# A static tile of 128 rows per expert between the passes of a switch-routed MoE, with a hint for the code of the next pass

## The chip, the cores and the metric

The kernel runs on one core of one Trainium2 chip. The metric is the device time of one execution in microseconds; of the kernel before there are three timed runs, 733.85, 734.2 and 734.55 us, and one further execution that the hardware profiler recorded.

## The reference

Attention with a band and a few global keys, and behind it a mixture of experts that sends each token to one expert. All data are f32.

```python
# attention: B 4, H 8, S 768, D 64; keys 0..7 are global, else the last 96
scores = q @ k.T / sqrt(D) + bias        # bias = -slope[h] * distance
a = softmax(where(keep, scores, -1e9))
x = (a @ v).transpose(0, 2, 1, 3).reshape(3072, 512)
# experts: E 8, DM 512, F 1024
expert_idx = argmax(x @ w_gate, axis=1)
gate_w = softmax(x @ w_gate)[arange(N), expert_idx]
for e in range(E):
    mask = expert_idx == e
    out[mask] = gate_w[mask, None] * (maximum(x[mask] @ w1[e], 0) @ w2[e])
```

How many of the 3072 tokens go to which expert is known only on the chip, at run time.

## The kernel before

The first 207 us or so are the attention (`banded`). It leaves every block of tokens in rows `xr` together with the routing logits `lg`; `choose` and `dispatch` pick the expert of each token and scatter the rows into `xs_dram`, sorted by expert (L205, POOL). The weights of experts 0 and 1 (2 MB each for w1 and w2) are loaded by SP into two slots while the attention is still running (`fetch`, L718).

The experts' work comes in two kinds.

*Static tiles* have exactly 128 rows and the same code whatever the routing. `x_in_s` transposes the gathered rows into `xsT` (PE L762, DVE L763), `up_s` makes 64 matmuls of 128 columns (PE L771) with two relu's on ACT (L775), `down_s` makes 16 matmuls of 512 columns (PE L781), a multiplication by the gate on DVE (`ys`, L783) and one scatter to the output on POOL (L728). Before, only experts 0 and 1 have such a tile, and both are worked off ahead of the passes, under the tail of the dispatch.

*Passes* take the remaining rows of each expert, all experts in turn (`passes`). A pass is a switch over 14 widths, 0, 128, 160 and so on to 512 columns; for every width there is a body of code of its own, and PE, ACT, DVE and POOL each jump to the body whose number stands in the table `form`. SP has no switch. A body (`one_pass`) has an up phase, 8 groups of 8 matmuls (as the trace records them: two for each f32 matmul of the program) into `ph` (PE L874) with a relu into `hT` on ACT (L876), and a down phase, 4 times 16 recorded matmuls into `py` (PE L881; four 128-column blocks `d` of the output, 8 chunks `f` each), a copy to `yT` on ACT (L883), and `back`: transposes on PE (L862) and gated copies into `y` on DVE (L864, L868). At its end POOL scatters `y` to the output (L728). In between the body transposes the next expert's gathered rows (`x_in`, PE L840, DVE L841), up to four tiles of 128, the last of them just before the last `back`, and `x_meta` takes over token numbers and gates on DVE (L845, L847). With this run's tokens the widths are 352, 288, 384, 416, 384, 416, 416 and 288 for experts 0 to 7.

Behind each pass come the gathers of the expert after next on POOL (`gathers`, L721) and its weights on SP (`fetch`). Behind pass 0 there is also `judge`, one small matmul (L952) whose result decides at the very end whether a general path has to do the work again; it never does here.

PE's order of work is that of the program text (a manual schedule for PE); the other engines' instructions are placed by the scheduler, so that gathers for later passes may stand further ahead than in the text. At the head of each body of a switch a hint names the place behind the switch.

Of the kernel before, what the change touches and what calls it, by code (L numbers as in the profile page):

```python
# [9 lines left out]
F32 = mybir.dt.float32  # L10
# [10 lines left out]
def kernel(  # L21
# [659 lines left out]

    NS = 2
    TP = 4
# [3 lines left out]
    class Experts:  # L687
        def __init__(self, stack, rt, psum):
            self.rt = rt
            ps_s, ps_t, ps_o, ps_r = self.psum = psum  # L690
            self.wpool = stack.enter_context(tc.tile_pool(name="wpool", bufs=1))
            self.pool = stack.enter_context(tc.tile_pool(name="tab", bufs=1))
            self.w1 = [self.wpool.tile([P, NDC, F], F32, name=f"w1_{i}") for i in range(2)]
            self.w2 = [self.wpool.tile([P, NFC, DM], F32, name=f"w2_{i}") for i in range(2)]
# [4 lines left out]
            self.grow_s = T([P, NS], I32, name="grow_s")  # L699
            self.inv_s = T([P, NS], I32, name="inv_s")  # L700
# [4 lines left out]
            self.xs = [T([P, XW], F32, name=f"xs{i}") for i in range(NS)]  # L705
            self.xsT = [T([P, NDC, P], F32, name=f"xsT{i}") for i in range(NS)]
            self.hsT = T([P, NFC, P], F32, name="hsT")
            self.ys = T([P, DM], F32, name="ys")
            self.tos = T([P, NS], I32, name="tos")
# [26 lines left out]
        def early(self):  # L736
# [4 lines left out]
            inv = T([P, NS], F32, name="inv_sf")  # L741
            nc.vector.tensor_scalar(inv[:], cnt[:], iota_p[:, 0:1], None, ALU.is_le)
            row = T([P, NS], F32, name="row_s")
            nc.vector.tensor_scalar(row[:], ebase[:, 0:NS], iota_p[:, 0:1], None, ALU.add)
            nc.vector.scalar_tensor_tensor(self.grow_s[:], inv[:], float(2 ** 22), row[:], ALU.mult, ALU.add)
            nc.vector.tensor_scalar(self.inv_s[:], inv[:], float(2 ** 30), None, ALU.mult)
# [8 lines left out]
            for j in range(NS):  # L755
                self.gather(self.xs[j][:], self.grow_s[:, j:j + 1])


        def x_in_s(self, j):
            pt = self.t[j % 2]  # L760
            for c in range(NDC):
                nc.tensor.transpose(pt[:, c, :], self.xs[j][:, ts(c, P)], ident[:])  # L762
            nc.vector.tensor_copy(out=self.xsT[j][:], in_=pt[:])  # L763
            nc.vector.tensor_tensor(self.tos[:, j:j + 1], self.xs[j][:, DM + 1:DM + 2].bitcast(I32),
                                    self.inv_s[:, j:j + 1], ALU.bitwise_or)

        def up_s(self, j):
            for f in range(NFC):
                ph = self.ph[f // 4 % 2][:, 0, :]
                for c in range(NDC):  # L770
                    nc.tensor.matmul(ph[:, ts(f % 4, P)], lhsT=self.w1[j][:, c, ts(f, P)],  # L771
                                     rhs=self.xsT[j][:, c, :], start=(c == 0), stop=(c == NDC - 1),
                                     skip_group_check=True)
# [4 lines left out]
        def down_s(self, j):  # L778
            py = self.py[j % 2]
            for f in range(NFC):  # L780
                nc.tensor.matmul(py[:], lhsT=self.hsT[:, f, :], rhs=self.w2[j][:, f, :],  # L781
                                 start=(f == 0), stop=(f == NFC - 1))
            nc.vector.tensor_scalar(self.ys[:], py[:], self.xs[j][:, DM:DM + 1], None, ALU.mult)  # L783
            self.scatter(self.ys[:], self.tos[:, j:j + 1])


        def begin(self, stack):

            ps_s, ps_t, ps_o, ps_r = self.psum
            pool = stack.enter_context(tc.tile_pool(name="pass", bufs=1))  # L790
            self.xg = [pool.tile([P, TP, XW], F32, name=f"xg{i}") for i in range(2)]
# [7 lines left out]
            self.t = [ps_t.tile([P, TP, P], F32, tag="t", name=f"pt{i}") for i in range(2)]  # L799
# [3 lines left out]
        def clear(self, i):  # L803
            nc.vector.memset(self.xg[i][:], 0.0)

        def table(self):
# [8 lines left out]
            nc.vector.tensor_scalar(self.inv_i[:], inv[:], float(2 ** 30), None, ALU.mult)  # L815

            steps_i = T([P, E], I32, name="steps_i")
            nc.vector.scalar_tensor_tensor(steps_i[:], cnt[:], float(GN - 1), self.lim[:],  # L818
                                           ALU.add, ALU.subtract)
            nc.vector.tensor_scalar(steps_i[:], steps_i[:], GN.bit_length() - 1, None,  # L820
                                    ALU.logical_shift_right)
            steps = T([P, E], F32, name="steps")
# [26 lines left out]
        def one_pass(self, e, n, between):  # L849

            w1t, w2t, xT, hT, y = self.w1[e % 2], self.w2[e % 2], self.xT[e % 2], self.hT, self.y[e % 2]
# [26 lines left out]
            for d in range(NDC if n else 0):  # L878
# [7 lines left out]
                if d == 1:  # L886
# [9 lines left out]
        def passes(self, after_first):  # L896
            PEs = (PE, mybir.EngineType.Activation, mybir.EngineType.DVE, mybir.EngineType.Pool)
            _, forms = nc.values_load_multi_w_load_instructions(
                self.form[0:1, 0:E], engines=PEs, min_val=0, max_val=len(WIDTHS) - 1,
                skip_runtime_bounds_check_because="the table has no other forms")  # L900
            for e in range(E):
                index = {eng: forms[e] for eng in PEs}
                for i in tc.Switch(index, len(WIDTHS)):
                    more = []
                    if e + 1 < E:
                        self.x_meta(e + 1)
                        more = [lambda: (self.x_in(e + 1, 0), self.x_in(e + 1, 1)),
                                lambda: self.x_in(e + 1, 2), lambda: self.x_in(e + 1, 3)]
                    self.one_pass(e, WIDTHS[i], more)
                if e + 2 < E:  # L910
                    self.gathers(e + 2)
                    self.fetch(e + 2)
                if e == 0:
                    after_first()
# [4 lines left out]
    with ExitStack() as stack, tc.manual_schedule(engines={PE}):  # L919
# [8 lines left out]
        ex.clear(0)  # L928
# [29 lines left out]
    with tc.If(flag > 0):  # L958
# [36 lines left out]
```

## Time and profile before

| | |
|---|---|
| timed runs, median of 3 | 734.2 us (733.85 to 734.55) |
| profiled execution | 733.7 us |
| its span | 731.9 us |
| mean granted TensorE clock | 0.928 |
| PE busy | 578.0 us, 4093 instructions |
| DVE, ACT, POOL busy | 178.2, 126.1, 103.8 us |

The span is the time from the first to the last recorded instruction; 1.8 us of the execution lie around it. PE, DVE, ACT and POOL are the engines for matmuls, vector work, activations and general work; PEld is PE's weight load, SP issues most of the loads. "Busy" counts instructions that do work; an engine that waits for another is idle, and where the profile shows nothing that it waited for, the idle time is put down to "issue". Busy PE says nothing about its speed, which is why the granted clock is given beside it.

### The profile page before, as it was taken

The page shows a single profiled execution, that of the slowest core. Times are in us where ns is not written, and L with a number is a line of the kernel's source. Part 1 is how long each engine was busy: PE and PEld are TensorE (multiplying, and loading weights), DVE is VectorE, ACT ScalarE, POOL GpSimd, SP SyncE. Part 2 cuts the span into 40 slices and gives each one's busy share as a digit, 9 for nine tenths or more (in the row PEclk, how much of TensorE's full clock was granted, in tenths as well). Part 3 has the DMA queues.
Part 4 walks back from the last instruction along what each step waited for, and adds up shares of the span by engine and source line. Part 5 has one row for each costly group of instructions (what it writes and reads, how often), then busy time and mean ns, then how long its engine had stood idle before and what let it go on. Part 6 is the DMA issues. An engine that isn't in the chain of part 4 may idle for free.

```text
span 731.9 us, 10117 instructions
## 1 busy us (share of the span) xinstructions
PE 578.0 (79%) x4093; PEld 389.7 (53%) x4093; DVE 178.2 (24%) x499; ACT 126.1 (17%) x225; POOL 103.8 (14%) x148
## 2 busy tenths in 40 slices
PE   3898697997999499489489499948948985896890
PEld 2786576785876256357245345524524552454660
DVE  6565555664660101101101100110110020011010
ACT  1444243533410010010010011001001100100100
POOL 2002203105006300210300120040021002002001
PEclk9999999999999699789799889979979997998995
DMA  8888975566104203413603422060351304001001
GB/s 188 234 249 222 274 193 155 141 157 183 37 2 151 79 0 116 158 46 116 191 6 116 155 55 83 33 212 0 116 162 32 114 22 149 0 1 52 0 4 36
DMA packets 98473, 77.49 MB, mean 106 GB/s; under 512 B 79355, under 2 KB 79355, under 8 KB 98305
## 3 DMA queue, kind: packets, MB, share of 16 engines
q1 hardware_dynamic: 90240, 56.63, 26.7%
q0 software_dynamic: 6704, 18.98, 7.9%
q8 instruction: 56, 0.92, 0.6%
q14 instruction: 113, 0.92, 0.5%
q10 hardware_dynamic: 1360, 0.04, 0.1%
HBM read 61.45 MB, written 12.89 MB: 102 GB/s over the span
## 4 chain that ended last, share of the span: by engine, by line
PE 67%; issue 15%; DVE 8%; ACT 3%; DMA 2%; POOL 1%; ACTq 1%; another core or an unknown queue 0%; DVEq 0%; POOLq 0%
PE ph L874 25%; PE py L881 22%; PE po L358 4%; PE sp L336 4%; ACT hT L876 2%; PE pt L225 2%; PE pt L862 2%; PE pr L369 2%; PE pt L840 2%; PE px L380 2%; DVE p L347 2%; DMA xs_dram<-xr,slot_i 1%; DVE y L864 1%; PE pr L374 1%; PE ph L771 1%
## 5 line engine op out<-in xcount | busy, mean ns | idle before, releaser
L874 PE MATMUL ph<-xT,w 128*128 128x416 f32 (+3 forms) x512 | 188.0, 523 | 80.3 <-issue 60.7
L874 PEld LDWEIGHTS ph<-xT,w 128*128 128x128 f32 x512 | 103.6, 209 | 162.0 <-issue 97.8
L881 PE MATMUL py<-hT,w 128*128 128x416 f32 (+3 forms) x512 | 162.3, 473 | 0.0
L881 PEld LDWEIGHTS py<-hT,w 128*128 128x128 f32 x512 | 95.5, 190 | 55.5 <-issue 27.7
L728 POOL DMA_INDIRECT out_dram<-y,to x27 | 26.3, 976 | 393.4 <-DVE y L868 293.0
L876 ACT ACTIVATE hT<-ph 128x416 f32<-128x416 f32 (+3 forms) x64 | 30.5, 477 | 269.0 <-PE ph L874 253.7
L348 ACT ACTIVATE p<-p 128x1024 f32<-128x1024 f32 (+1 forms) x48 | 47.0, 983 | 86.8 <-DVE p L347 79.6
L841 DVE COPY xT<-pt 128x512 f32<-128x512 f32 x32 | 21.2, 685 | 165.9 <-PE pt L840 165.9
L864 DVE TENSOR_TENSOR y<-pt,gate 128x384 f32<-128x384 f32 (+1 forms) x32 | 16.3, 508 | 181.0 <-PE pt L862 180.9
L347 DVE SCALAR_TENSOR_TENSOR p<-sp,other 128x1024 f32<-128x1024 f32 x40 | 47.5, 1216 | 13.3 <-remote 9.8
L336 PE MATMUL sp<-qt,kt 64*128 64x128 f32 x448 | 40.5, 292 | 10.4 <-DVE p L347 7.2
L358 PE MATMUL po<-p,vt 128*64 128x128 f32 x448 | 41.2, 284 | 5.7 <-issue 5.6
L883 ACT COPY yT<-py 128x416 f32<-128x416 f32 (+3 forms) x32 | 14.9, 465 | 165.5 <-PE py L881 165.5
L336 PEld LDWEIGHTS sp<-qt,kt 64*128 64x128 f32 x448 | 33.4, 203 | 11.9 <-issue 11.2
L721 POOL DMA_INDIRECT xg<-xs_dram,grow x32 | 32.6, 1020 | 34.4 <-issue 33.8
L358 PEld LDWEIGHTS po<-p,vt 128*64 128x64 f32 x448 | 28.5, 142 | 8.6 <-issue 8.6
L205 POOL DMA_INDIRECT xs_dram<-xr,slot_i x24 | 23.8, 990 | 38.9 <-DVE steps_i L818 30.4
L840 PE MATMUL pt<-ident,xg 128*128 128x128 f32 x128 | 19.1, 285 | 10.2 <-DVE xT L841 4.7
L336 PE MATMUL sp<-qt,ka 64*128 64x128 f32 x256 | 26.6, 285 | 0.0
L358 PE MATMUL po<-p,va 128*64 128x128 f32 x256 | 25.7, 279 | 0.0
L369 PE MATMUL pr<-p,one_in 128*32 128x128 f32 x704 | 24.2, 276 | 0.0
L840 PEld LDWEIGHTS pt<-ident,xg 128*128 128x128 f32 x128 | 15.3, 146 | 15.0 <-DVE y L868 5.6
(148 smaller groups left out, 421.3 us busy)
## 6 DMA issues: line engine op xcount, KB each, us to landing
w<-in_moe_w_dram SPq DMA_DIRECT2D x32, 1024.0 KB, 6.4
raw_q<-in_q_dram SPq DMA_DIRECT2D x24, 256.0 KB, 3.2
raw_k<-in_k_dram SPq DMA_DIRECT2D x24, 256.0 KB, 4.0
vt<-in_v_dram SPq DMA_DIRECT2D x24, 256.0 KB, 3.8
va<-vt SPq DMA_DIRECT2D x16, 192.0 KB, 3.6
va<-vt SPq DMA_DIRECT2D x16, 64.0 KB, 3.0
xg<-xs_dram,grow POOLq DMA_INDIRECT x32
out_dram<-y,to POOLq DMA_INDIRECT x27
```

Of the source, the lines that this page charges most:

```text
L205: d = nc.gpsimd.indirect_dma_start(out=xs_dram[:], out_offset=bass.IndirectOffsetOnAxis(ap=slot_i[:, u:u + 1], axis=0), in_=xr[:, u, :].bi ...
L336: nc.tensor.matmul(sp[:, a, j, t, :], lhsT=kt[r, 2 * g + j, :], rhs=qts[n][r, 2 * g + j, :], start=True, stop=True, skip_group_check=True)
L347: nc.vector.scalar_tensor_tensor(z, sc, QS, bi, ALU.mult, ALU.add)
L348: nc.scalar.activation(z, z, AF.Exp)
L358: nc.tensor.matmul(po[D * a:D * a + D, m, :], lhsT=vt[:, 2 * m + a, :], rhs=ps[n][m // 2][:, a, m % 2, t, :], start=(x == 0), stop=(x == l ...
L369: nc.tensor.matmul(pr[GW * m:GW * m + GW, 0, :], lhsT=one_in[:, a, :], rhs=ps[n][m // 2][:, a, m % 2, t, :], start=(x == 0), stop=False, s ...
L721: nc.gpsimd.indirect_dma_start(out=dst.bitcast(I32), out_offset=None, in_=xs_dram[:], in_offset=bass.IndirectOffsetOnAxis(ap=idx, axis=0), ...
L728: d = nc.gpsimd.indirect_dma_start(out=out[:], out_offset=bass.IndirectOffsetOnAxis(ap=idx, axis=0), in_=src, in_offset=None, bounds_check ...
L840: nc.tensor.transpose(pt[:, c, :], x[:, t, ts(c, P)], ident[:])
L874: nc.tensor.matmul(ph, lhsT=w1t[:, c, ts(f, P)], rhs=xT[:, c, 0:n], start=(c == 0), stop=(c == NDC - 1), skip_group_check=True)
L876: nc.scalar.activation(hT[:, f, 0:n], ph, AF.Relu)
L881: nc.tensor.matmul(py, lhsT=w2t[:, f, ts(d, P)], rhs=hT[:, f, 0:n], start=(f == 0), stop=(f == NFC - 1), skip_group_check=True)
```

## The change

The passes hold at most 384 columns (`TP` 4 to 3, ten widths in place of 14), and every expert has a static tile of 128 rows (`lim` starts at 128). So with this run's tokens the passes of experts 2 to 7 become 128 columns narrower: 256, 288, 256, 288, 288 and 160; experts 0 and 1 keep theirs.

The static tile of expert e+2 stands between pass e and pass e+1, for e = 0 to 4 with both halves. Behind pass 5 there are `up_s` of expert 7 and the judge, behind pass 6 `down_s` of expert 7. Its rows are transposed within pass e (`x_in_s` as a third piece between the down groups, after the third). Ahead of each static tile `hint` writes, on PE and on ACT, a hint for the body that the next switch will take; for pass 0 the hint stands in front of the static tile of expert 1. DVE and POOL have no such hint.

There is a third weight slot. Expert 2 is loaded ahead of the passes, and behind pass e the weights of expert e+3 follow in place of e+2's. Two memsets (`clear`) go from DVE to POOL and in front of the static work. The static tiles' gates are copied when the rows are transposed (`gates`), and `steps` is kept from falling below zero. The If at the end has its general path as the far block.

```diff
     NS = 2
-    TP = 4
+    TP = 3
...
-            nc.vector.memset(self.lim[:], 0.0)
+            nc.vector.memset(self.lim[:], float(P))
...
         def fetch(self, e):
-            for dst, src, n in ((self.w1[e % 2], moe_w1, NDC), (self.w2[e % 2], moe_w2, NFC)):
+            w1t, w2t = self.w[e % 3]
+            for dst, src, n in ((w1t, moe_w1, NDC), (w2t, moe_w2, NFC)):
...
         def clear(self, i):
-            nc.vector.memset(self.xg[i][:], 0.0)
+            nc.gpsimd.memset(self.xg[i][:], 0.0)
...
-                if d == 1:
+                if d in (1, 2):
                     other()
...
+        def hint(self, e):
+            index = {eng: self.forms[e] for eng in self.ENGINES[:2]}
+            tc.switch_hint(index, len(WIDTHS), label=f"pass{e}")
+
+        def passes(self, judge):
             for e in range(E):
-                index = {eng: forms[e] for eng in PEs}
-                for i in tc.Switch(index, len(WIDTHS)):
+                index = {eng: self.forms[e] for eng in self.ENGINES}
+                for i in tc.Switch(index, len(WIDTHS), hint=f"pass{e}"):
                     more = []
                     if e + 1 < E:
                         self.x_meta(e + 1)
-                        more = [lambda: (self.x_in(e + 1, 0), self.x_in(e + 1, 1)),
-                                lambda: self.x_in(e + 1, 2), lambda: self.x_in(e + 1, 3)]
+                        more.append(lambda: (self.x_in(e + 1, 0), self.x_in(e + 1, 1)))
+                        more.append(lambda: self.x_in(e + 1, 2))
+                    if e + NS < E:
+                        more.append(lambda: self.x_in_s(e + NS))
                     self.one_pass(e, WIDTHS[i], more)
+                if e + 3 < E:
+                    self.fetch(e + 3)
                 if e + 2 < E:
                     self.gathers(e + 2)
-                    self.fetch(e + 2)
-                if e == 0:
-                    after_first()
+                if e + 4 < E:
+                    self.gather_s(e + 4)
+                if e + 1 < E:
+                    self.hint(e + 1)
+                if e + 3 < E:
+                    self.up_s(e + 2)
+                    self.down_s(e + 2)
+                elif e + 2 < E:
+                    self.up_s(e + 2)
+                    judge()
+                elif e + 1 < E:
+                    self.down_s(e + 1)
...
-        ex.clear(0)
+        for i in range(2):
+            ex.clear(i)
         ex.x_in_s(0)
         ex.up_s(0)
         dispatch(pool, ex.t[0][:].rearrange("p t c -> p (t c)"), rt, xr, oh)
         ex.table()
         ex.gathers(0)
-        ex.clear(1)
         ex.gathers(1)
         ex.x_in_s(1)
+        for e in (2, 3):
+            ex.gather_s(e)
+        ex.fetch(2)
         ex.down_s(0)
         ex.up_s(1)
+        ex.load_forms()
+        ex.hint(0)
         ex.down_s(1)
...
-    with tc.If(flag > 0):
+    with tc.If(flag > 0, preferred_fallthrough_block=False):
```

On PE, before, the piece from the end of the widest body of pass 1 over the switch of pass 2 to the head of its first body (`py`, `pt` and `ph` are PSUM tiles, `w_1` the second weight slot; `SWITCH_STRIDE` and the two `ISA` rows are the switch, L903 and L990 its lines):

```order
L881 MATMUL py_2923<-hT,w_1_134 128x512 x8
L862 MATMUL pt_2920<-ident,yT_2910 128x128 x4
L840 MATMUL pt_2921<-ident,xg_2905 128x128 x4
L862 MATMUL pt_2921<-ident,yT_2911 128x128 x4
L990 UNCONDITIONAL_BRANCH
L990 SWITCH_STRIDE
L990 ISA x2
L903 BRANCH_PREFETCH_HINT
```

The pass ends with a fourth tile of input transposes and goes straight into the next switch.

On PE, in the change, the same place, behind pass 1 (L786 is `up_s`, L796 `down_s`, L775 `x_in_s`, L858 `x_in`, L881 now `back`, L900 the down matmul, L924 the hint):

```order
L881 MATMUL pt_2924<-ident,yT_2914 128x128 x3
L775 MATMUL pt_2924<-ident,xs_145 128x128 x4
L900 MATMUL py_2926<-hT,w_1_134 128x384 x8
L881 MATMUL pt_2923<-ident,yT_2913 128x128 x3
L881 MATMUL pt_2924<-ident,yT_2914 128x128 x3
L1034 UNCONDITIONAL_BRANCH
L924 SWITCH_STRIDE
L924 ISA
L924 BRANCH_PREFETCH_HINT
L786 MATMUL ph_2921<-xsT_147,w_0_131 128x128 x16
L786 MATMUL ph_2922<-xsT_147,w_0_131 128x128 x16
L796 MATMUL py_2926<-w_0_132,hsT 128x512 x8
```

Between the end of the pass and the next switch (which follows these rows) stand the hint and the static tile; the input transposes at the end are gone, and those of the static tile share `pt_2924` with the `back` ahead of them.

On SP, in the change, from the attention's last loads into the passes (L723 is the weight load, `w_2` the third slot):

```order
L264 DMA va<-vt 96x512
L265 DMA va<-vt 32x512
L723 DMA w_2_2906<-in_moe_w_dram 128x2x1024 x2
L723 DMA w_2_2907<-in_moe_w_dram 128x4x512 x2
L1034 UNCONDITIONAL_BRANCH
L723 DMA w_0_131<-in_moe_w_dram 128x2x1024 x2
L723 DMA w_0_132<-in_moe_w_dram 128x4x512 x2
```

The first two weight rows stand ahead of the passes and are new; each later load is the whole of one expert behind one pass.

## Rows read from the trace of the kernel before

**Rows 1.** The page, part 1: busy time and share of each engine.

```profile
PE 578.0 (79%) x4093; PEld 389.7 (53%) x4093; DVE 178.2 (24%) x499; ACT 126.1 (17%) x225; POOL 103.8 (14%) x148
```

**Rows 2.** The page, part 4: the chain that ended last, by engine.

```profile
PE 67%; issue 15%; DVE 8%; ACT 3%; DMA 2%; POOL 1%; ACTq 1%; another core or an unknown queue 0%; DVEq 0%; POOLq 0%
```

**Rows 3.** Waits from 200 us on: engine, line, releaser, total us, times, longest.

```profile
PE ph L874 <- issue: 60.7, 9, 8.6
```

**Rows 4.** The chain in order of time: start us, us, what.

```profile
208.60 7.41 PE ph L771 x64
...
216.78 6.88 PE py L781 x16
...
351.88 7.89 issue
...
692.57 2.21 PE ph L874 x8
```

**Rows 5.** Timeline, pass 7's first matmuls: start us, us, what, idle before.

```profile
673.64 4.17 PE L874 MATMUL ph<-xT,w 128*128 128x288 f32 x8 [5.12 <-issue]
```

**Rows 6.** Timeline, end of pass 1, SP: start, us, what.

```profile
348.89 0.93 SPq L718 DMA_DIRECT2D w<-in_moe_w_dram  x2
```

**Rows 7.** Windows of 10 us around two entries: PE, PEld, DVE, ACT, POOL, clock, DMA, GB/s.

```profile
351.00:361.00 10.00, 1.39 (x4) 0.84 (x3) 0.67 (x2) 0.00 (x0) 3.24 (x4) 0.62 0.82 267
669.00:679.00 10.00, 4.73 (x10) 3.01 (x11) 0.37 (x2) 0.41 (x1) 3.82 (x4) 0.66 0.30 95
```

**Rows 8.** DMA queues from 347 to 362 us: packets, MB, share.

```profile
q8 instruction: 3, 0.05, 1.6%
```

**Rows 9.** Windows of passes 0, 1 and 3, columns as in rows 7.

```profile
245.90:298.97 53.07, 44.78 (x157) 27.96 (x157) 4.86 (x12) 5.51 (x12) 0.60 (x1) 0.92 0.17 55
298.97:351.16 52.19, 39.70 (x157) 28.98 (x157) 5.67 (x15) 4.88 (x12) 8.07 (x8) 0.87 0.34 110
...
411.80:477.46 65.66, 52.36 (x162) 28.26 (x160) 5.79 (x13) 6.16 (x12) 7.10 (x7) 0.92 0.28 91
```

**Rows 10.** Lines by form from 200 us, PE: busy us, mean ns, idle before.

```profile
L881 PE MATMUL py<-hT,w 128*128 128x416 f32 x192 | 68.5, 512 | 0.0
...
L881 PE MATMUL py<-hT,w 128*128 128x288 f32 x128 | 32.0, 406 | 0.0
```

**Rows 11.** The same, ACT.

```profile
L876 ACT ACTIVATE hT<-ph 128x416 f32<-128x416 f32 x24 | 12.4, 517 | 106.0 <-PE ph L874 106.0
...
L876 ACT ACTIVATE hT<-ph 128x288 f32<-128x288 f32 x16 | 6.6, 410 | 55.9 <-PE ph L874 55.9
```

**Rows 12.** Timeline, end of pass 1 (288 columns): start, us, what, idle before.

```profile
340.11 0.66 PE L840 MATMUL pt<-ident,xg 128*128 128x128 f32 x4 [0.77 <-DVE y L868]
...
350.64 0.52 PE L862 MATMUL pt<-ident,yT 128*128 128x128 f32 x3 [1.02 <-DVE xT L841]
```

**Rows 13.** Timeline of pass 7, its last transposes and a scatter.

```profile
711.50 0.55 PE L862 MATMUL pt<-ident,yT 128*128 128x128 f32 x3 [0.22 <-ACT yT L883]
...
714.07 0.98 POOL L728 DMA_INDIRECT out_dram<-y,to  x1 [0.30 <-issue]
```

**Rows 14.** Timeline, the way out of pass 0 and into pass 1.

```profile
298.92 0.10 PEld L952 LDWEIGHTS <-ones 128*128 128x128 bf16 x1 [0.21 <-issue]
...
306.12 0.16 DVE L953 TENSOR_SCALAR bad_i<-py 128x1 int32<-128x1 f32 x1 [6.44 <-issue]
...
307.51 4.18 PE L874 MATMUL ph<-xT,w 128*128 128x288 f32 x8 [8.40 <-issue]
```

**Rows 15.** Timeline and window ahead of the passes: memset, dispatch, first scatter; 230 to 245.9.

```profile
210.42 1.78 DVE L804 MEMSET xg<- 128x2064 f32 x1 [0.66 <-issue]
...
215.84 0.19 PE L187 MATMUL pt<-oh,before 128*128 128x48 bf16 x1
...
218.05 1.04 POOL L205 DMA_INDIRECT xs_dram<-xr,slot_i  x1 [30.40 <-DVE steps_i L818]
...
230.00:245.90 15.90, 10.51 (x40) 5.99 (x38) 3.58 (x7) 0.60 (x1) 11.28 (x12) 0.84 0.48 132
```

More of the change, by code (lines that the diff above doesn't have):

```diff
@@ L692, in __init__ @@
             self.pool = stack.enter_context(tc.tile_pool(name="tab", bufs=1))
-            self.w1 = [self.wpool.tile([P, NDC, F], F32, name=f"w1_{i}") for i in range(2)]
-            self.w2 = [self.wpool.tile([P, NFC, DM], F32, name=f"w2_{i}") for i in range(2)]
+            self.w = [self.slot(self.wpool, i) for i in range(NS)]
             T = self.pool.tile
@@ L740, in early @@
             nc.vector.tensor_scalar(self.lim[:, 0:NS], cnt[:], float(P), None, ALU.min)
[L741 to L746, printed above, removed]
+            self.rows_s(cnt, 0, NS)
             shape = [P, E, TP]
@@ L754, in early, with rows_s, gather_s, x_in_s @@
                                     ebase[:].unsqueeze(2).to_broadcast(shape), ALU.add)
[L755 to L760, printed above, removed]
-            for c in range(NDC):
[L762 to L767, printed above, removed]
+            for e in range(NS):
+                self.gather_s(e)
+        def rows_s(self, cnt, a, b):
+            n = b - a
+            inv = self.pool.tile([P, n], F32, name=f"inv_s{a}")
+            nc.vector.tensor_scalar(inv[:], cnt[:], iota_p[:, 0:1], None, ALU.is_le)
+            row = self.pool.tile([P, n], F32, name=f"row_s{a}")
+            nc.vector.tensor_scalar(row[:], ebase[:, a:b], iota_p[:, 0:1], None, ALU.add)
+            nc.vector.scalar_tensor_tensor(self.grow_s[:, a:b], inv[:], float(2 ** 22), row[:],
+                                           ALU.mult, ALU.add)
+            nc.vector.tensor_scalar(self.inv_s[:, a:b], inv[:], float(2 ** 30), None, ALU.mult)
+        def gather_s(self, e):
+            self.gather(self.xs[e % 2][:], self.grow_s[:, e:e + 1])
+        def x_in_s(self, e):
+            x, pt = self.xs[e % 2], self.t[e % 2]
+            for c in range(NDC):
+                nc.tensor.transpose(pt[:, c, :], x[:, ts(c, P)], ident[:])
+            nc.vector.tensor_copy(out=self.xsT[e % 2][:].rearrange("p c t -> p (c t)"),
+                                  in_=pt[:].rearrange("p c t -> p (c t)"))
+            nc.vector.tensor_tensor(self.tos[:, e:e + 1], x[:, DM + 1:DM + 2].bitcast(I32),
+                                    self.inv_s[:, e:e + 1], ALU.bitwise_or)
+            nc.vector.tensor_copy(out=self.gates[:, e:e + 1], in_=x[:, DM:DM + 1])
+        def up_s(self, e):
             for f in range(NFC):
@@ L770, in up_s @@
                 for c in range(NDC):
-                    nc.tensor.matmul(ph[:, ts(f % 4, P)], lhsT=self.w1[j][:, c, ts(f, P)],
-                                     rhs=self.xsT[j][:, c, :], start=(c == 0), stop=(c == NDC - 1),
+                    nc.tensor.matmul(ph[:, ts(f % 4, P)], lhsT=self.w[e % 3][0][:, c, ts(f, P)],
+                                     rhs=self.xsT[e % 2][:, c, :], start=(c == 0), stop=(c == NDC - 1),
                                      skip_group_check=True)
@@ L790, in begin @@
             pool = stack.enter_context(tc.tile_pool(name="pass", bufs=1))
+            self.w.append(self.slot(pool, NS))
             self.xg = [pool.tile([P, TP, XW], F32, name=f"xg{i}") for i in range(2)]
@@ L798, in begin @@
             self.ph = [ps_s.tile([P, 2, 512], F32, tag="s", name=f"ph{i}") for i in range(2)]
-            self.t = [ps_t.tile([P, TP, P], F32, tag="t", name=f"pt{i}") for i in range(2)]
+            self.t = [ps_t.tile([P, 4, P], F32, tag="t", name=f"pt{i}") for i in range(2)]
             self.py = [ps_o.tile([P, 512], F32, tag="o", name="py0"),
@@ L849, in one_pass @@
         def one_pass(self, e, n, between):
-            w1t, w2t, xT, hT, y = self.w1[e % 2], self.w2[e % 2], self.xT[e % 2], self.hT, self.y[e % 2]
+            w1t, w2t = self.w[e % 3]
+            xT, hT, y = self.xT[e % 2], self.hT, self.y[e % 2]
             between = list(between)
```

39 lines of the change are left out of this document (22 added, 17 removed).

## The prediction

> **What bounds the kernel now.** I read the page first, for who is busy, then the chain that ended last, for who is waited for, and only then single stretches. PE is busy for 578.0 us of 731.9 [rows 1], and in the chain PE has 67% and "issue" 15% [rows 2]: after PE's own arithmetic the largest item is time in which PE waits for nothing that the profile shows. The table of waits puts 60.7 us of it at one place, L874 behind "issue", nine waits, the longest 8.6 us [rows 3]. L874 opens a pass, so this is the way into the eight passes. It comes in two sizes: the chain has 7.89 us of it in front of pass 2 [rows 4], the timeline 5.12 us in front of pass 7 [rows 5]. What differs is the traffic: two 1 MB weight loads are issued at 348.89, just ahead of pass 2 [rows 6], and the DMA share around that entry is 0.82, against 0.30 around pass 7, which no load precedes [rows 7]. In the stretch around the entry of pass 2, PE's instruction queue q8 fetched three packets, 0.05 MB [rows 8]. So I read the stop as the wait for the code of the chosen width.
>
> Each entry has a second price. The first 8 matmuls of pass 7 take 4.17 us [rows 5], the last 8 of its up phase, of the same width, 2.21 [rows 4]; the granted clock over the entry's ten microseconds is 0.66 [rows 7], a mean of the lower of the two levels (1.2 GHz) and the higher (2.4), after PE had stood still. That is 2.0 us per entry, at eight entries 16. Pass 1 has a second slow group (its clock is 0.87, the others' 0.92 [rows 9]); I put 1.7 us on that. The entries thus hold 60.7 + 16 + 1.7 = **78.4 us** of the run, and all other terms of this change turn out small beside them.
>
> **The sum.** The base is the profiled execution, 733.7 us (span 731.9 and 1.8 around it); it lies 0.5 below the median of 734.2.
>
> 1. *Narrower passes.* Experts 2 to 7 get a static tile, so their passes lose 128 columns. L881 takes 512 ns at 416 columns and 406 at 288 [rows 10]: 106 ns x 128 matmuls (64 up, 64 down) = 13.6 us a pass. Whole passes agree: 65.66 us at 416 and 52.19 at 288 [rows 9]. Six passes: **-81.6**. ACT's hT is shorter too, 517 to 410 ns [rows 11], on which PE waits five times a pass, and each of four back transposes has one part less, 7.41/64 = 0.12 us [rows 4]: 0.5 + 0.5 = 1.0, six times **-6**.
> 2. *Static tiles.* Six more, at 7.41 us for 64 up matmuls and 6.88 for 16 down [rows 4]: 14.3 each, **+85.7**. So the matmuls alone give nothing: the tile takes up what the passes lose, and 4 us more.
> 3. *Input transposes.* The fourth x_in at the end of a pass goes. It made the last back transposes wait 1.02 us behind DVE's copy [rows 12]; without it, in pass 7, they waited 0.22 [rows 13]. Seven times 0.8 = **-5.6**; seven pieces of 4 transposes go and six come (x_in_s), **-0.5**. The new piece shares its buffer with a back transpose in every second pass; such a piece waited 0.77 for DVE [rows 12]: three times, **+2.3** (0 to 4.6).
> 4. *The join.* The static tile's first matmul on PE follows the last DVE y of the pass: in the rows DVE ends at 351.88 and PE at 351.17 [rows 4, 12]. PE used to sit that out within the entry; now it stands by itself, seven times 0.7, **+4.9**.
> 5. *More jumps.* Hints, and the switch that stays: leaving pass 0 cost PE 0.21 us where nothing was missing [rows 14]. I count two such steps at each of eight entries, **+3.2** (0 to 6).
> 6. *Ends.* Pass 7 shrinks to 160 columns, two scatters at the end instead of three, 0.98 + 0.30 us apart [rows 13]: **-1.3**. The third slot's 4 MB load now runs beside the dispatch's scatters and the first gathers; bounds 0 and 4, I take **+1.5**, near the lower end, since that stretch has a DMA share of 0.48 without it [rows 15].
> 7. *Nothing.* The two memsets leave DVE (1.78 us each) for POOL: POOL idles 30.40 us ahead of its first scatter, and DVE's chain was covered by PE's up matmuls until L187 at 215.84 [rows 15]. If that cover were gone it would be 3.6 us. POOL and DVE still enter a switch without a hint (6.44 us for DVE at an exit, L953 [rows 14]); their first work of a pass is needed after its up phase, which is eight groups of 2.21 us at 288 columns [rows 4] and, by columns, some 10 us at 160. ACT is hinted like PE, and PE can run four groups of 8 ahead of it. The judge's matmul costs the same wherever it stands.
>
> Together: 733.7 - 81.6 - 6 + 85.7 - 5.6 - 0.5 + 2.3 + 4.9 + 3.2 - 1.3 + 1.5 = **736.3**, with every entry as before. What decides is how much of the 78.4 us the hint and the cover of a static tile take away.
>
> **What the hint is worth** has no row of its own. The nearest rows are at the other end of a pass, where the code already holds one hint, at the head of each width. PE leaves pass 0 in 0.21 us; DVE, with its own hint, stands for 6.44 us at the same exit [rows 14]. Between hint and exit PE had some 150 matmuls, DVE 12 instructions (the window of pass 0 counts 157 and 12 [rows 9]). So a hint can be served wholly or not at all, by what lies between. The new hint has the static tile's 80 matmuls between itself and the entry: between the two. Bounds: all entries free, 736.3 - 78.4 = 657.9; none free. I take **half of them**. One that isn't served costs 5.12 us without a load running and 8.40 with one [rows 5, 14], mean 6.8, and 2.2 for the clock after it (2.0, and pass 1's share): 9.0. The loads (4 MB at each of five pass ends, at the 267 GB/s of [rows 7] 15.7 us) run as long as the static tile, so the entry meets their tail, between the two ends. Four times 9.0 = 36: 657.9 + 36 = **693.9**; from four times 7.1 (no load) to four times 10.6 it is 686 to 700, and with one entry more or less 679 to 711.
>
> **Rivals.**
> - *All served.* PE alone bounds, 657.9; with the bounds of terms 3, 5 and 6, 651 to 667. For it: the exit's 0.21 us, and a static tile of 14.3 us is longer than any of the stops [rows 3]. Against it: DVE's exit.
> - *None served* (the change doesn't do what it says). The entries merely move behind the static tile, where loads are over or nearly: eight times 7.1 is 657.9 + 57 = 715, with five of them at 10.6 it is 732. For it: DVE's exit, and the eight stops [rows 3], each in front of a width chosen at run time. Beside these rows, the Trainium skill ("Runtime: NRT & Kernel Launch", section "Instruction fetch mechanics") says that code is prefetched only in sequence and that a taken branch outside the two pages held must wait for its page; it has no hint. The trace agrees at the entries and disagrees at PE's exit.
> - *Slower.* The tile's own code gets in the way: PE comes out of a pass into code that isn't there, while the loads just issued hold the DMA queues, and stops at the front of the tile for 8.4 us and 2.2 of clock; and the entry behind it misses as well. Six tiles times 10.6 = 64 on top of 715: 779. It decides from 734 on, that is, when stops eat 76 of the 78.4 us: seven stops at 10.6, or eleven at 7.1, of the fifteen places. For it: the static code sits behind ten widths of body, and the loads start exactly there. Against it: at PE's exit of pass 0, with two loads issued at its end too, nothing was missing.
>
> **How the numbers follow.** Half served 0.50, all 0.27, none 0.14, slower 0.06, 0.03 for what I don't see. The forecast is the likeliest, 694. Its own range is 679 to 711. From 652 to 716 the range takes in most of "all served" and the lower end of "none", and leaves out some 0.18. A measurement here can't tell changes under 0.2% (1.5 us) from none. Faster by more than that: nearly all of the first three cases, 0.90; within it, 0.03 (the upper end of "none", at 732, touches it); slower 0.07.
>
> **What would show it.** In the profile after: L874's line (new number) behind "issue" well below 60.7 us, but not gone, with some entries under 1 us and some at 5 or more; pass 3, at 288 columns, near 40 us from its first matmul to its last (52.19 less 8.4 for the entry, 2.0 and 1.7 for the clock, by [rows 9]); each static tile near 14.3 us, with 0.7 behind DVE in front of it; PE's busy time lower by the clock's share at most, under 20 us from 578.0, so that the gain is mostly idle time; mean clock above 0.93. Wrong would be: stops inside or in front of the static tiles (rival three), entries all alike (rival one or two), or a sum that fails without entries, say PE waiting for weights (xT or w) that the third slot brings late.

## The result and the profile after

| | before | after |
|---|---|---|
| timed runs, median | 734.2 us | 667.55 us (665.21 to 675.04, 4 runs) |
| ratio | | 0.911, 95% interval 0.9038 to 0.9181 |
| profiled execution | 733.7 us | 667.69 us |
| its span | 731.9 us | 665.5 us |
| mean granted clock | 0.928 | 0.965 |

The change makes the kernel 9% faster. The forecast was 694, its range 652 to 716 holds the time, but the case that the forecast took for the likeliest had a range of its own, 679 to 711, and that does not. The time lies just above the upper end of the rival in which no entry is left, 651 to 667. (By the bounds that the prediction names for its terms 3, 5 and 6, that end comes to 665.5: 657.9 + 2.3 + 2.8 + 2.5.)

The page of the kernel after, parts 1, 2 and 4: busy time, the granted clock in 40 slices, and the chain by engine, beside [rows 1, 2].

```profile
PE 563.6 (85%) x4541; PEld 434.8 (65%) x4541; DVE 176.4 (27%) x520; ACT 125.2 (19%) x237; POOL 104.4 (16%) x148
...
PEclk9799899999999989999998999999999999899995
...
PE 70%; DVE 9%; issue 8%; ACT 4%; DMA 3%; POOL 2%; another core or an unknown queue 1%; ACTq 0%; POOLq 0%; DVEq 0%
```

PE has 448 more instructions and is busy for 14.4 us less. That fits the lower clock at the entries, which the prediction put at 16 + 1.7 us; it was not measured apart. "issue" fell from 15% to 8% of the chain. Part 5 of the same page has the first matmuls of a pass, now L893, and the static tiles', L786 (busy us, mean ns, idle before):

```profile
L893 PE MATMUL ph<-xT,w 128*128 128x288 f32 (+3 forms) x512 | 131.1, 408 | 20.1 <-ACT hT L895 19.3
...
L786 PE MATMUL ph<-xsT,w 128*128 128x128 f32 x512 | 61.2, 281 | 9.1 <-issue 3.7
```

The 60.7 us behind "issue" of [rows 3] are gone as a whole: what L893 still waits is ACT's hT, but for 0.8 us. The chain in time, from the end of pass 0 to the first group of pass 1, and then the tile behind pass 1 (start, us, what):

```profile
293.54 0.56 PE pt L881 x3
294.46 0.35 DVE y L887
294.90 7.38 PE ph L786 x64
302.28 6.87 PE py L796 x16
309.15 1.95 PE ph L893 x8
...
349.85 2.81 PE ph L786 x23
352.65 2.35 issue
355.00 6.47 PE ph L786 x41
```

Pass 1 follows the tile's last matmul without a gap, at full clock: 1.95 us for its first 8 matmuls. The tile itself costs 7.38 + 6.87 us, as in [rows 4]. The second tile shown has a stop of 2.35 us inside, and half the clock for part of what follows. Two places are left where an entry or its like is seen. The first is pass 6, which has only `up_s` and the judge in front of it (timeline, PE and ACT):

```profile
572.26 2.19 PE L893 MATMUL ph<-xT,w 128*128 128x288 f32 x8
...
576.12 0.41 ACT L895 ACTIVATE hT<-ph 128x288 f32<-128x288 f32 x1 [3.02 <-issue]
...
576.58 5.84 PE L893 MATMUL ph<-xT,w 128*128 128x288 f32 x16 [2.13 <-ACT hT L895]
```

PE was there at once. ACT stood for 3.02 us, 1.67 of them after PE's first 8 matmuls had ended; PE waited 2.13 us for it and lost clock. The other place is the end, PE's last transposes and POOL's last scatters, beside [rows 13]:

```profile
643.04 0.44 PE L881 MATMUL pt<-ident,yT 128*128 128x128 f32 x2 [0.22 <-ACT yT L902]
...
645.38 0.87 POOL L733 DMA_INDIRECT out_dram<-y,to  x1 [0.31 <-issue]
650.32 0.98 POOL L733 DMA_INDIRECT out_dram<-ys,tos  x1 [4.07 <-issue]
```

The last scatter is not one of pass 7's but that of the last static tile: POOL issues it behind pass 7, after a jump of its own.

### The profile page after: what moved, and what is told of

It reads as the page before. It is cut to its first block, busy times and chain, and to the rows that moved or that the text cites. A ratio compares the mean times of both kernels' runs of the same rounds, so it can differ in the third digit from the quotient of the medians.

```text
span 665.5 us, 11159 instructions
## 1 busy us (share of the span) xinstructions
PE 563.6 (85%) x4541; PEld 434.8 (65%) x4541; DVE 176.4 (27%) x520; ACT 125.2 (19%) x237; POOL 104.4 (16%) x148
## 4 chain that ended last, share of the span: by engine, by line
PE 70%; DVE 9%; issue 8%; ACT 4%; DMA 3%; POOL 2%; another core or an unknown queue 1%; ACTq 0%; POOLq 0%; DVEq 0%
PE ph L893 19%; PE py L900 18%; PE ph L786 8%; PE py L796 6%; PE po L358 4%; PE sp L336 4%; DVE p L347 2%; PE pr L369 2%; ACT hT L895 2%; PE pt L225 2%; PE px L380 2%; DMA xs_dram<-xr,slot_i 2%; PE pt L858 2%; PE pt L881 1%
## 5 line engine op out<-in xcount | busy, mean ns | idle before, releaser
L893 PE MATMUL ph<-xT,w 128*128 128x288 f32 (+3 forms) x512 | 131.1, 408 | 20.1 <-ACT hT L895 19.3
L893 PEld LDWEIGHTS ph<-xT,w 128*128 128x128 f32 x512 | 93.6, 194 | 58.5 <-ACT hT L895 33.0
L900 PE MATMUL py<-hT,w 128*128 128x288 f32 (+3 forms) x512 | 121.3, 393 | 0.0
L900 PEld LDWEIGHTS py<-hT,w 128*128 128x128 f32 x512 | 92.3, 190 | 21.3
L786 PE MATMUL ph<-xsT,w 128*128 128x128 f32 x512 | 61.2, 281 | 9.1 <-issue 3.7
L786 PEld LDWEIGHTS ph<-xsT,w 128*128 128x128 f32 x512 | 59.6, 196 | 11.6 <-issue 10.6
L895 ACT ACTIVATE hT<-ph 128x288 f32<-128x288 f32 (+3 forms) x64 | 25.4, 397 | 180.7 <-PE ph L893 177.7
L796 PE MATMUL py<-w,hsT 128*128 128x512 f32 x128 | 56.3, 593 | 0.6 <-issue 0.6
L883 DVE TENSOR_TENSOR y<-pt,gate 128x256 f32<-128x256 f32 (+1 forms) x32 | 13.1, 408 | 119.5 <-PE pt L881 118.9
L358 PE MATMUL po<-p,vt 128*64 128x128 f32 x448 | 39.9, 277 | 4.7 <-issue 4.7
L796 PEld LDWEIGHTS py<-w,hsT 128*128 128x128 f32 x128 | 23.7, 190 | 27.6 <-issue 27.6
L902 ACT COPY yT<-py 128x288 f32<-128x288 f32 (+3 forms) x32 | 12.3, 385 | 130.7 <-PE py L900 130.7
L726 POOL DMA_INDIRECT xg<-xs_dram,grow x24 | 24.6, 1024 | 14.4 <-issue 6.1
```

The lines of the kernel that those rows point to most:

```text
L358: nc.tensor.matmul(po[D * a:D * a + D, m, :], lhsT=vt[:, 2 * m + a, :], rhs=ps[n][m // 2][:, a, m % 2, t, :], start=(x == 0), stop=(x == l ...
L726: nc.gpsimd.indirect_dma_start(out=dst.bitcast(I32), out_offset=None, in_=xs_dram[:], in_offset=bass.IndirectOffsetOnAxis(ap=idx, axis=0), ...
L786: nc.tensor.matmul(ph[:, ts(f % 4, P)], lhsT=self.w[e % 3][0][:, c, ts(f, P)], rhs=self.xsT[e % 2][:, c, :], start=(c == 0), stop=(c == ND ...
L796: nc.tensor.matmul(py[:], lhsT=self.hsT[:, f, :], rhs=self.w[e % 3][1][:, f, :], start=(f == 0), stop=(f == NFC - 1))
L893: nc.tensor.matmul(ph, lhsT=w1t[:, c, ts(f, P)], rhs=xT[:, c, 0:n], start=(c == 0), stop=(c == NDC - 1), skip_group_check=True)
L895: nc.scalar.activation(hT[:, f, 0:n], ph, AF.Relu)
```

## The experiments

Two theories were to be told apart. **Cover:** the wait for the code of a width is as long as before, but PE still has the tile's matmuls in hand when it begins, and so it isn't seen. **Hint:** the code is there in time because it was announced.

### Without any hint, and with the first alone

```diff
-                for i in tc.Switch(index, len(WIDTHS), hint=f"pass{e}"):
+                for i in tc.Switch(index, len(WIDTHS)):
...
-                if e + 1 < E:
-                    self.hint(e + 1)
...
-        ex.hint(0)
```

> The change without any hint, all else kept. Theory A (cover): in the change's trace PE has no idle time in front of passes 1 to 5 and 7 because the 16 long matmuls of down_s are still queued when the jump waits for its code; so passes 1 to 7 start as in the change, only pass 0, which has no cover, gets its stop of some 4.2 us back, and the two stops inside static tiles (2.35 and 1.33 us, with about 2 us of clock) either go, if the hints cause them, or stay: 666 to 672 us. Theory B (hint): without it each of passes 1 to 7 stops again for 5.1 to 8.4 us and loses 2.0 of clock: 667.6 + 7 x 7.1 to 7 x 10.6 = 717 to 742 us.

In e2_hint0 the line `ex.hint(0)` stays, and the hint of the first switch with it.

> The change with the hint for pass 0 alone. Theory A (cover): pass 0 starts as in the change, passes 1 to 7 too; if the later hints cause the stops inside the static tiles, 2.35 + 1.33 us and some 2 us of clock go: 661 to 668 us. Theory B (hint): 7 stops come back, 717 to 742 us less nothing for pass 0, so 713 to 738 us. Against e1_no_hint the difference is pass 0's hint alone, some 4 to 6 us by either theory.

Measured: 665.12 us (ratio to before 0.9064, 0.8986 to 0.9141) without any, 665.39 us (0.9074, 0.8986 to 0.9161) with the first. Neither can be told from the change; e1_no_hint is 1 us under the cover theory's range, e2_hint0 within it, and both are some 50 us under the hint theory's. The table of waits of e1_no_hint has for L893 and for the tiles' L786 behind "issue" (us, times, longest), and its timeline shows the two of L893, in front of passes 0 and 6:

```profile
PE ph L893 <- issue: 5.5, 2, 3.4
...
PE ph L786 <- issue: 2.4, 2, 1.7
```

```profile
248.03 4.09 PE L893 MATMUL ph<-xT,w 128*128 128x352 f32 x8 [3.42 <-issue]
...
572.58 2.20 PE L893 MATMUL ph<-xT,w 128*128 128x288 f32 x8 [2.12 <-issue]
```

So six of the eight entries are free without a hint: those with a `down_s` directly in front of them (pass 0 has transposes that wait for DVE in between). The hint theory falls for them.

The cover can be seen directly, since the trace also records PE's branch, the jump itself (view of the switch's line: ns, start; PEldq is PE's sequencer). First into pass 1 of e1_no_hint, then into pass 2 of the change:

```profile
L1031 PEldq COMPARE_BRANCH  x1: 3745/3745/3745, 304.7 to 304.7; - x1
```

```profile
L1034 PEldq COMPARE_BRANCH  x1: 412/412/412, 362.5 to 362.5; - x1
```

In e1_no_hint the tile's last matmul ends at 310.57, 5.8 us after this branch began and 2.1 after it was done. All of its eight branches take 3.5 to 4.4 us; the six behind a `down_s` begin 5.8 us or more before the tile's last matmul ends, those of passes 0 and 6 only 0.8 and 1.8. In the change three take 0.41 to 0.49 us (passes 0, 2 and 6), the other five 3.3 to 4.3: on PE three of eight hints were served, and where one wasn't the tile hid the wait.

What hints do is seen in the other two. In pass 6 PE's stop of 2.12 us is there without a hint and not with it, but ACT was late in its place. In pass 0 the first hint takes the stop away; e2_hint0's timeline of PE:

```profile
244.89 5.06 PE L893 MATMUL ph<-xT,w 128*128 128x352 f32 x8 [0.78 <-DVE xT L859]
```

These are 2.6 us of stop in the trace, of which 1.0 goes again in the first group (5.06 us against 4.09), and too few for the medians to show. Of the stops inside the tiles the one of 1.33 us (tile of expert 4) is absent without the hints; the tile of expert 3 keeps one of 1.66 us, and the tile of expert 7 gets one of 0.76. So they aren't the hints' alone (see the last section).

### No tiles: what the cover is worth

```diff
-                if e + 3 < E:
-                    self.up_s(e + 2)
-                    self.down_s(e + 2)
-                elif e + 2 < E:
-                    self.up_s(e + 2)
-                    judge()
-                elif e + 1 < E:
-                    self.down_s(e + 1)
+                if e == E - 3:
+                    judge()
```

> The change without hints and without the static tiles between the passes (up_s and down_s of experts 2 to 7 are left out, so 768 rows are not computed; their input transposes, gathers and weight loads stay). It measures what a static tile costs in its place. Theory A (cover): the entries are open again, so of 6 x 14.3 = 85.8 us that go, 7 x 7.1 to 7 x 10.6 = 50 to 74 us come back: 665.1 - 85.8 + 50 to 74 = 629 to 654 us, with L893 behind issue near 5 to 8 us per pass. Theory B (the entries got cheap for another reason, such as narrower passes, fewer widths or later loads): the whole of the tiles' time goes: 579 to 590 us.

The hints are left out too, so e1_no_hint is what it is compared with; 768 rows are not computed, so this is no version to use. Measured: 642.92 us (0.8776, 0.8745 to 0.8807), within the cover theory's range and 53 us above the other's. The table of waits and, from the timeline, the entry into pass 3:

```profile
PE ph L893 <- issue: 55.7, 9, 8.7
```

```profile
400.86 1.78 PE L893 MATMUL ph<-xT,w 128*128 128x288 f32 x3 [8.71 <-issue]
```

The stops are back, as long as in [rows 3], with ten widths, narrower passes and a third slot; none of these had made the entries cheap. Six tiles of 14.25 us cost 665.12 - 642.92 = 22.2 us in their places, 3.7 each. The other 63 us are time in which PE would have stood still (50.2 us, 55.7 less the 5.5 of e1_no_hint) or run at the lower clock.

The cover isn't all. PE's branch into pass 3 is twice as long here as behind a tile:

```profile
L1025 PEldq COMPARE_BRANCH  x1: 8138/8138/8138, 392.5 to 392.5; - x1
```

Into passes 1 to 5 it takes 7.6 to 8.1 us, where e1_no_hint has 3.5 to 3.9. So some 4 us of each of these five waits are gone behind a tile without any cover, and the tile's matmuls hide the rest; the 5.8 us that they cover would not have hidden 8. What shortens the wait was not tested; the loads, issued with the end of the pass, are some 10 us further on when the branch behind a tile begins.

The rule cited with rival two (the Trainium skill, "Runtime: NRT & Kernel Launch", section "Instruction fetch mechanics") agrees with this run: without cover every jump into a width waits.

### The other order: short matmuls in front of the switch

```diff
+                if 0 < e < E - 1:
+                    self.down_s(e + 1)
+                if e + 2 < E:
+                    self.up_s(e + 2)
+                if e == E - 3:
+                    judge()
...
-                if e + 3 < E:
-                    self.up_s(e + 2)
-                    self.down_s(e + 2)
...
```

> The change with the two halves of a tile in the other order: behind pass e first down_s(e+1), whose up_s stood a pass earlier, then up_s(e+2), so that 64 short matmuls of 0.116 us stand in front of the switch in place of 16 long ones of 0.43 us. Same work, same hints. Theory A (cover): what PE has queued is worth some 1.6 us in place of 5.8, so each of passes 1 to 6 is late by 2 to 3 us, as pass 6 is in the change already, and loses about 2 us of clock: five new late entries, 667.6 + 5 x 4 to 5 x 5 = 688 to 693 us. Theory B (hint): the code has come by hint whatever stands there, 667 to 672 us.

> e3_down_first (down_s of the tile before, then up_s) without any hint. In e3_down_first's trace four of passes 1 to 6 had PE there at once and ACT late by 2.4 us. Theory A, as it now stands: short queued matmuls cover 1.6 us of a wait for code of some 3.7, so without hints PE is late by some 2 us at every entry, but ACT is late there anyway, so little is added: 679 to 684 us. Theory B (the hint is what counts where cover is short): the entries cost PE what they cost before the change, 5.1 us and more each, and the clock: 679 + 4 x 5 to 4 x 7 = 699 to 707 us.

Measured: 679.42 us (0.9244, 0.9178 to 0.9311) with hints and 679.22 us (0.9223, 0.9184 to 0.9263) without. For e6_down_first_no_hint that is within the cover theory's range. For e3_down_first it is between the two expectations, and neither was right: PE was on time in front of passes 2, 3, 5 and 6, as the hint theory had it (2.73 and 1.65 us late in front of 1 and 4), and the kernel was slower, as the cover theory had it. The timeline of e3_down_first around pass 3, PE and ACT, tells why:

```profile
414.12 2.11 PE L893 MATMUL ph<-xT,w 128*128 128x288 f32 x8
419.75 4.15 PE L893 MATMUL ph<-xT,w 128*128 128x288 f32 x16 [3.52 <-ACT hT L895]
```

```profile
416.25 0.60 ACT L790 ACTIVATE hsT<-ph 128x512 f32<-128x512 f32 x1 [4.84 <-PE ph L893]
419.29 0.41 ACT L895 ACTIVATE hT<-ph 128x288 f32<-128x288 f32 x1 [2.44 <-issue]
```

The tile now ends with a relu on ACT, so ACT jumps last and its own 2.44 us stand open; the relu before them starts late as well (416.25, with the tile's last matmul ended by 414.3). PE waits 3.52 us for it all. In the change ACT's last relu ends 6 us ahead of pass 1 (302.98 against 308.99). Without hints PE is late as well, in e6_down_first_no_hint's table of waits and in front of pass 3:

```profile
PE ph L893 <- issue: 13.7, 6, 3.0
```

```profile
424.05 2.20 PE L893 MATMUL ph<-xT,w 128*128 128x288 f32 x8 [2.28 <-issue]
```

Against 8.71 us with nothing in front and none with 16 long matmuls, 64 short ones leave 2.28. PE's branch shows why:

```profile
L1029 PEldq COMPARE_BRANCH  x1: 4003/4003/4003, 419.9 to 419.9; - x1
```

It begins 1.9 us before the tile's last matmul ends, in place of 5.8, and takes as long as behind long matmuls. What counts is the time of the last instructions before the jump, not the length of the tile. The hints take most of PE's 13.7 us away (5.0 are left in e3_down_first), and the time doesn't change, since ACT is late at the same place.

### The input transposes alone, in the kernel before

```diff
-                if d == 1:
+                if d in (1, 2):
                     other()
```

> The kernel before with one thing of the change: the fourth tile of input transposes moves from the end of the pass to behind the third down group (d in (1, 2)). By term 3 of the prediction the last back transposes wait 0.22 us in place of 1.02, seven times 0.8 = 5.6 us: 728 to 729 us. Rival: the entry behind it starts to wait for its code when DVE's last y is done and not when PE is, so only part or nothing comes through: 732 to 734 us.

Measured: 733.91 us, ratio 0.9989 (0.9961 to 1.0017): nothing. The rival has the number but not the reason. The table of waits of the kernel before, and then that of e4_before_x_in (us, times, longest):

```profile
PE pt L862 <- DVE xT L841: 7.3, 7, 1.1
...
PE pt L840 <- DVE y L868: 4.2, 5, 0.9
...
PE pt L840 <- DVE y L864: 1.3, 2, 0.7
```

```profile
PE pt L840 <- DVE y L868: 8.5, 10, 0.9
...
PE pt L840 <- DVE y L864: 2.6, 4, 0.7
PE pt L862 <- ACT yT L883: 1.9, 8, 0.3
```

The wait at the end of the pass fell from the 1.02 of [rows 12] to 0.24 each, and the moved transposes wait in their new place for DVE, with which they share a buffer: 8.5 + 2.6 us where the kernel before has 4.2 + 1.3. The 5.6 us are given back to the last tenth, and the entries wait no longer than before (59.1 us behind "issue" in all, against 60.7).

### Versions that repair what is left

The first takes the last scatter into pass 7, moves one relu to DVE and keeps two hints (before passes 0 and 6).

```diff
-                if f % 4 == 3:
+                if f == NFC - 1 and e == E - 1:
+                    nc.vector.tensor_scalar(self.hsT[:, f - 3:f + 1, :].rearrange("p a b -> p (a b)"), ph,
+                                            0.0, None, ALU.max)
+                elif f % 4 == 3:
...
+                    if e + 1 == E:
+                        more.append(lambda: self.scatter(self.ys[:], self.tos[:, e:e + 1]))
...
-                    self.down_s(e + 1)
+                    self.down_s(e + 1, scatter=False)
```

> A version meant to beat both: the change with hints for passes 0 and 6 alone, the scatter of the last static tile issued by POOL inside pass 7 and not behind it, and the last relu of expert 7's tile on DVE, so that ACT can go into pass 6 early. In the trace of e2_hint0 the last scatter starts 5.2 us after the one before it (term 6 had forecast a shorter end) and pass 6 starts 2.25 us late and then runs at the lower clock for some 1.7. Theory A (cover): with the scatter moved the end comes 4 to 5 us earlier; pass 6 starts on time on PE (in the change, with its hint, PE was there and ACT's hT was late), and ACT is there too: another 3 to 4 us. 665.4 - 8 = 656 to 658 us. Rival: POOL's scatter inside pass 7 finds DVE's product or POOL's own jump late, and the end waits for something else than the last scatter: 663 to 666 us.

Measured: 662.49 us (0.9023, 0.9001 to 0.9045), just under the rival's range; its interval still touches that of the change. Pass 6 does what was expected, and the last scatter too; pass 0 does not (timeline, PE, and POOL's last row):

```profile
247.47 4.18 PE L897 MATMUL ph<-xT,w 128*128 128x352 f32 x8 [3.17 <-issue]
...
573.17 2.19 PE L897 MATMUL ph<-xT,w 128*128 128x288 f32 x8
575.98 4.15 PE L897 MATMUL ph<-xT,w 128*128 128x288 f32 x16 [0.62 <-ACT hT L899]
```

```profile
642.53 0.88 POOL L733 DMA_INDIRECT out_dram<-y,to  x1 [0.30 <-issue]
```

The last scatter now starts 1.9 us behind PE's end in place of 6.8, but the span ends 16.5 us behind its end where it was 14.2 in the change: some 2 us of the 5 are lost to what comes after it, which the profile doesn't name. And pass 0 stops for 3.17 us although its hint stands where it stands in e2_hint0, with the same rows of PE between hint and switch.

The second edit gives the static tiles' `ys` a second buffer, in the change (e9_two_ys) and together with the first (e8_tail_relu_two_ys).

```diff
-            self.ys = T([P, DM], F32, name="ys")
+            self.ys = [T([P, DM], F32, name=f"ys{i}") for i in range(2)]
...
-            nc.vector.tensor_scalar(self.ys[:], py[:], self.gates[:, e:e + 1], None, ALU.mult)
+            nc.vector.tensor_scalar(self.ys[e % 2][:], py[:], self.gates[:, e:e + 1], None, ALU.mult)
```

> The change with two buffers for the static tiles' product ys in place of one. In the change's trace DVE's second ys waits 6.83 us for the scatter of the first to land, and the copies of pass 0's inputs stand behind it; PE waits 5.56 us for them just ahead of pass 0. This wait was in the kernel before too (6.15 us), and the prediction left it as it was. Theory: the wait is a buffer's, so pass 0 starts at 241 and not at 246 us: 667.6 - 4.8 = 662 to 664 us. Rival: pass 0 then meets something else that is late, the gathers or the code of its width, whose hint has less time: 665 to 668 us.

> e5_tail_relu and the two buffers of e9_two_ys together; meant to beat all versions. If the three savings are of different stretches and add up: 662.5 - 4.8 = 657 to 659 us. Rival: the code of pass 0, late by 3.17 us in e5_tail_relu though its hint stood where it stands in e2_hint0 (there 0.78 us), now is late by more, since the wait for DVE no longer covers part of it: 660 to 662 us.

Measured: 661.83 us (0.9026, 0.8993 to 0.9058) and 658.98 us (0.8982, 0.8951 to 0.9013). The first lies within its theory's range, but its interval still overlaps the change's; the second is faster than the change beyond both intervals, and has the lowest median of the versions that compute all rows. DVE's wait in the change, and then DVE and PE of e9_two_ys at the same place:

```profile
242.76 0.75 DVE L798 TENSOR_SCALAR ys<-py,gates 128x512 f32<-128x512 f32 x1 [6.83 <-DMA out_dram<-ys,tos]
```

```profile
237.40 0.75 DVE L798 TENSOR_SCALAR ys<-py,gates 128x512 f32<-128x512 f32 x1 [0.86 <-issue]
...
241.37 0.69 DVE L859 COPY xT<-pt 128x512 f32<-128x512 f32 x1 [2.03 <-remote]
```

```profile
242.12 5.06 PE L893 MATMUL ph<-xT,w 128*128 128x352 f32 x8 [2.66 <-issue]
```

The wait for the buffer is gone, and pass 0 starts at 242.12 where it started at 246.06. Not all of the 6.83 us came through: the third copy starts 1.9 us after PE's transposes ended (239.45). The profile puts the 2.66 us in front of pass 0 down to "issue", but the copy ends at 242.06 and PE starts 0.06 behind it, and PE's branch there takes 0.48 us, so it is this copy and not the code; in e8_tail_relu_two_ys the row names it. The rival there, late code, is not seen.

```profile
243.43 5.06 PE L897 MATMUL ph<-xT,w 128*128 128x352 f32 x8 [2.17 <-DVE xT L863]
```

## Why the prediction was right or wrong

**The views and the bound: right.** The entries held what the chain said. 60.7 us behind "issue" went to nothing, the mean clock rose from 0.928 to 0.965, and the matmuls gave nothing, as terms 1 and 2 have it: a static tile took 14.25 us (14.3 forecast), and pass 3, from its first matmul to its last, 39.9 us (near 40 forecast). PE's busy time fell by 14.4 us, within the 20 named.

**The step that failed** is "One that isn't served costs 5.12 us without a load running and 8.40 with one", and with it the 36 us for four open entries. Half of the hints served was near what the traces show, three of eight on PE, but the other five cost PE nothing in front of the pass. The step put the price of the entry behind the tile at what it is behind the end of a pass, and asked only whether the hint comes in time. The rows of the two ends differ in another thing: behind the end of a pass PE had run dry, three transposes after a wait for DVE (1.02 us, [rows 12]); behind a static tile it has long matmuls, 0.43 us each, still in hand. The branch begins 5.8 us before they end (behind the end of a pass, in e7_no_tiles, 0.1 to 0.3 us after PE's last matmul), takes about half as long as there, and was hidden as a whole, hint or not: e1_no_hint has six of eight entries free, e7_no_tiles has them all back, 55.7 us. So none of the 36 us was due, and rival one has the number for a reason that it didn't give: it said "all served". Rival two was right that hints needn't be served, and wrong that the entries then "merely move behind the static tile". The argument from [rows 14], PE's 0.21 us at an exit with 150 matmuls and DVE's 6.44 with 12 instructions, was laid to the hint's distance. With the same rows of PE between hint and entry, pass 2 of the change was served and passes 1, 3, 4 and 5 were not. The time between may count: in pass 2, whose tile stops, the branch follows the hint by 13.2 us, in the other four by 8.6 to 10.2. But pass 6 was served after 6.2 us, and pass 0 of e5_tail_relu wasn't after 14.6. What serves a hint stays open.

**Terms of the sum.** From "all entries free", 657.9, to the profiled 667.7:

- Term 5, jumps: 3.2 forecast, 0 measured; L893 has no idle time but for ACT and, ahead of pass 0, for DVE. They lie under the same cover: -3.2.
- Term 6, ends: -1.3 forecast. From PE's last matmul to the end of the span it is 22.0 us where it was 19.9, since the last tile's scatter stands behind POOL's last pass: +3.5 against the forecast. The load beside the dispatch is small: POOL's first gather starts at 228.98 where it started at 228.34 (1.5 forecast, 0.6 measured): -0.9.
- Rival three exists in small: the tile of expert 3 takes 2.81 + 2.35 + 6.47 = 11.63 us up, where 7.38 is usual, that of expert 4 5.48 + 1.33 + 2.16 = 8.97: +4.3 and +1.6. It was foreseen at the front of the tile and with 8.4 us; it stands within it and is a quarter of that. The prediction had named stops inside the tiles as a sign of being wrong.
- Pass 6: ACT's late jump 1.7 and the lower clock 1.7 (5.85 against 4.16 us): +3.4. Term 7 had "PE can run four groups of 8 ahead of it"; PE waited after one.
- Pass 0 kept its 2.0 us of clock (4.66 against 2.63), behind a wait for DVE that was always there.

These make +10.7; the difference is 9.8, so 0.9 us are not assigned. Term 4, the join, was right: L786 waits for DVE 3.2 + 1.4 = 4.6 us (4.9 forecast). Term 3 came out in the change, where the last transposes wait 0.22 to 0.27; that the same move is worth nothing in the kernel before (e4_before_x_in) shows how near the two waits lie, of which the term counted the second for three passes only.

**What would show it:** "some entries under 1 us and some at 5 or more" was wrong: with the hints PE has none at 5, and none needs a hint but passes 0 and 6.

## What to carry to other kernels

PE paid for a jump's wait for code only from the moment at which it had nothing left in hand. So put independent work right in front of the jump, and end with the slowest instructions: 16 matmuls of 0.43 us hid all of a wait of 3.3 to 4.4 us, 64 of 0.116 left 1.7 to 3.0 us of one of 3.3 to 4.7. Look at every engine that jumps: in e3_down_first and in pass 6 of the change it was ACT, whose last instruction before the jump ended latest, that was late, and PE waited for it. And look for a wait that both kernels share: one more buffer moved the start of pass 0 by some 4 us in the trace, which no part of this change had touched.

## What was not expected

- The same hint, at the same place, with the same rows behind it, is served in one kernel and not in another: pass 0 stops 0.78 us (for DVE) in the change and in e2_hint0, 3.17 us behind "issue" in e5_tail_relu. PE's branch takes 0.48, 0.46 and 3.71 us there. Code further on differs, but e8_tail_relu_two_ys has the code of e5_tail_relu but for the second buffer, and there the branch takes 0.46. With one trace of each it is open whether it is the kernel or the single execution.
- Straight code stops too: PE halts 1.6 to 2.35 us inside the tile behind pass 1, where nothing jumps, with hints and without. In all six stops in the tiles of the change, e1_no_hint and e2_hint0, PE's instruction queue begins a packet of 16 KB 0.2 to 1.8 us before the stop, and PE goes on 1.3 to 1.5 us after it has landed (in the change, the packet from 352.44 to 353.55, the stop from 352.65 to 355.00). That points at code that came late, as rival three has it, but no run tested it, and it was not tried with the weights loaded at another time.
- What waits for PE's last instruction ahead of a switch can start late. In e9_two_ys DVE's copy starts 1.9 us after PE's transposes ended, where in the change, at the same place, it was 0.04 (245.27 to 245.31). In e3_down_first ACT's relu starts at 416.25, though the tile's last matmul ended by 414.3 and the pass's first 8 ran in between. The profile names no cause. Part of the 3.52 us in e3_down_first is this, then, and not ACT's own jump.
